# An annealed order of work, bf16 weight flips, clock-keeping matmuls and mixing by token pairs in a linear-attention and token-mixing kernel

## The chip, the cores and the metric

The kernel runs on one NeuronCore of a Trainium2 chip. The metric is the device time of one execution in microseconds (us); smaller is better. The engines are named as in the profile: PE (TensorE, matrix products), DVE (VectorE), ACT (ScalarE), POOL (GpSimd) and SP (SyncE, which here only issues DMAs).

## What is computed

Two layers follow each other. The first is a linear attention with a decaying state, for 4 batches, 8 heads, 768 tokens and 48 features per head; the second mixes tokens with two 768x768 matrices and channels with one 384x384 matrix.

```python
for t in range(S):                                   # attention, state is D x D per batch and head
    cur = np.einsum('bhd,bhe->bhde', u[None] * kt, vt)
    y[:, :, t] = np.einsum('bhd,bhde->bhe', rt, state + cur)
    state = w[None, :, :, None] * state + np.einsum('bhd,bhe->bhde', kt, vt)
x = y, heads side by side                            # (4, 768, 384)
theta = x @ w_theta
zr, zi = x * np.cos(theta), x * np.sin(theta)
y = np.einsum('ts,bsd->btd', w_tok_r, zr) + np.einsum('ts,bsd->btd', w_tok_i, zi)
u = x + y
out = u + np.maximum(u @ w_ch, 0.0)
```

## The kernel before

The 768 tokens of a batch are six chunks of 128, taken as three pairs; a pair of a batch is the unit of work, and there are 12 of them. The weights are loaded once.

For a batch, `heads` scales r by powers of w, two heads at a time (`Rw`, L492, on POOL, in batch 0 on DVE), and turns it with flips, which are PE transposes against an identity matrix (L473), into `RT`. For a pair, `attention` scales k into `Kw` (L520, POOL), flips it into `KT`, casts v to bf16 into `vb` (ACT), makes the scores (PE L543, on 64 rows of the array), masks them into `mAT` (DVE L548), makes `PD` (DVE L553) and from it the diagonal term `dg` (PE L561) and `yd` (POOL L568), carries the state along (PE L585 and L593, result `Sb`), and sums all into y (PE L627 and L632). DVE adds y and yd into `x` (L639). Then x is flipped to `xT`, theta is a product with `Wth` (PE L651), ACT makes sine and cosine (L655, L658), DVE makes `zr` (L661) and POOL `zi` (L664). All this is float32 where it is loaded or accumulated and bf16 where it is multiplied on PE.

`mixing` takes a pair of a batch once all of the batch's zr and zi are there: for each of its two chunks 12 products of 128x384 (PE L683, six with `WrT`, six with `WiT`), summed in one PSUM bank, then `un` (DVE L689), flips to `uT`, the channel product with `Wch` (PE L700), `fin` (DVE L704) and one store of 384 KB (SP L708).

The token weights come as rows and are needed as columns: each of the 12 row blocks (384 KB, float32) is flipped by six float32 transposes (PE L456) into a pair of banks, and copied to `WrT` or `WiT`.

PSUM has six slots in this kernel (`SLOTS`): two of two banks and four of one. Loads go into rings of SBUF buffers (ten `ld` buffers for k, v and weights, two `r_f` buffers for r). Nothing here is ordered by the programmer: `Plan` holds every step as a task with its dependencies, a priority, and an estimated duration on each engine that may run it; `Plan.order` plays the estimates forward, each engine taking the ready task of smallest priority, and the instructions are emitted in the resulting order. On the chip each engine, and SP's queue of DMAs, runs its instructions strictly in that order and waits on semaphores. An engine that waits holds up everything that stands behind it in its own order.

Of the kernel before, what the change touches and what calls it, by code (L numbers as in the profile page):

```python
# [22 lines left out]
SLOTS = (2, 2, 1, 1, 1, 1)  # L23


class Task:
    __slots__ = ("opts", "fn", "deps", "prio", "seq", "acq", "uses", "nwait", "users", "ready",
                 "start", "done", "end", "mode", "lock", "eng", "name")


class Plan:
# [7 lines left out]
    cold = 25000.0  # L39
# [6 lines left out]
    def add(self, opts, fn, rd=(), wr=(), prio=0.0, acq=(), use=(), mode=0, lock=False, name=""):  # L46
        t = Task()
        t.opts, t.fn, t.prio, t.mode, t.lock, t.name = opts, fn, prio, mode, lock, name
        t.seq = len(self.tasks)
# [24 lines left out]

    def pick_banks(self, acq, free, now, kept):
# [12 lines left out]
    def order(self):  # L88
        for t in self.tasks:
            t.users, t.nwait, t.ready = [], len(t.deps), {e: 0.0 for e in t.opts}  # L90
# [5 lines left out]
        def wake(t):  # L96
            for e in t.opts:
                waiting[e].append(t)
# [11 lines left out]
        while len(out) < n:  # L110
            for e in ENGINES:
                while free_at[e] <= now:
                    best, got = None, None
                    kept = set()
                    for t in sorted(waiting[e], key=lambda t: (t.prio, t.seq)):
                        if t.ready[e] > now or (t.lock and port > now):
                            continue
                        if len(t.opts) > 1:
                            mine = now + t.opts[e][0]
                            if any(max(free_at[o], t.ready[o], now) + t.opts[o][0] < mine  # L120
                                   for o in t.opts if o != e):
# [15 lines left out]
                    for o in t.opts:  # L137
                        waiting[o].remove(t)
# [4 lines left out]
                    if e == PE:  # L143
                        if t.mode != last_mode:
                            ns += 80.0
                        last_mode = t.mode
                        if now < self.cold:
                            ns *= 1.6
                    if t.lock:
# [39 lines left out]
def act_op(n, psum=True, ptr=False):  # L189
    return (n / 1.2 + (85 if psum else 100) + (90 if ptr else 0), 135)  # L190


def dve_op(n, rate=1.0):
    return (n / (0.96 * rate) + 70, 115)


def pool_op(n, rate=1.8):
    return (170 + rate * n, 100)


def pe_op(ns):
    return (ns, 215)
# [3 lines left out]
def kernel(  # L206
# [15 lines left out]
    ctx.enter_context(tc.manual_schedule())  # L222
    for t in P.order():
# [3 lines left out]
def build(ctx, tc, nc, r, k, v, w, u, moe_w_theta, moe_w_tok_r, moe_w_tok_i, moe_w_ch, out):  # L227
# [39 lines left out]
    pi2 = sb.tile([C, 1], F32, name="pi2")  # L267
    w_row = sb.tile([1, HD], F32, name="w_row")
# [39 lines left out]
    def setup():  # L308
# [6 lines left out]
        def fills(e):  # L315
            nc.vector.memset(ones, 1.0)
# [3 lines left out]
            for t in Sbs:  # L320
                nc.vector.memset(t, 0.0)
# [3 lines left out]
        P.add({DVE: (600, 100)}, fills, wr=["ones", "wu", "pi2", "uw", "bmask", "Sb0"], prio=-200)  # L325
# [81 lines left out]
    def load_r(b, parts=1):  # L407
        n = H // parts
        for i in range(parts):
            h = slice(i * n, (i + 1) * n)  # L410
            load(3500 / parts, r_fs[b % NR][:, h],
# [9 lines left out]
    def load_kv(b, pr, src):  # L421
        i = slot()
        for c in range(2):
            t0 = (2 * pr + c) * C
            load(1080, Ls[i][:, c, :, :D], src[b, :, t0:t0 + C, :].transpose([1, 0, 2]),
# [9 lines left out]
    def square(src, dst, key, prio, pos=None):  # L435
        s3 = src.rearrange("(o p) n -> p o n", p=C)
        for o, n in ((0, 2), (2, 1)):
            i = slot()
            load(560 * n, flat(i)[:, :n * HD].rearrange("p (o c) -> p o c", o=n),
# [324 lines left out]
```

## Time and profile before

| | |
|---|---|
| time, median of 3 runs | 161.48 us (159.95, 161.48, 161.77) |
| time of the profiled execution | 159.55 us |
| span of the profiled execution, first to last instruction | 157.8 us |
| busy time in that span: PE, DVE, ACT, POOL | 135.1, 110.0, 76.3, 75.6 us |
| moved by DMA | 25.0 MB, of which 20.06 MB read from HBM and 4.72 MB written |

The span is measured by the profiler from the first instruction to the last, and the execution's own time is 1.75 us longer. Matmuls are pipelined, so a PE that is shown busy can still be working slower than it could: a group of matmuls is better judged by the distance from its start to the start of the next group. The granted clock is the share of its full rate at which PE was let run, by the profiler's records.

### The profile page before, as it was taken

Reading aid. Unit: us, or ns where it says so; the run is one execution under the profiler, and the core shown is the slowest. Engines: PE = TensorE matmul, PEld = TensorE weight load, DVE = VectorE, ACT = ScalarE, POOL = GpSimd, SP = SyncE. Lnnn points to the kernel's source line nnn. Section 1 sums busy time; section 2 is a strip of 40 time slices with the busy share of each in tenths; the row PEclk is TensorE's granted clock in tenths of the full one; section 3 lists DMA queues with packets and bytes.
Section 4 is the critical chain, followed back from the end, with each engine's and each line's share of the span. In section 5 each row is a group of like instructions: output and inputs, shape, how many; then the busy total and the mean of one; then the engine's idle time right before and its main releaser. Section 6 shows DMA issues by size and latency. Waiting matters only on the chain.

```text
span 157.8 us, 3653 instructions
## 1 busy us (share of the span) xinstructions
PE 135.1 (86%) x1491; PEld 94.8 (60%) x1491; DVE 110.0 (70%) x158; ACT 76.3 (48%) x119; POOL 75.6 (48%) x61
## 2 busy tenths in 40 slices
PE   4068596788899999999979969999999999999950
PEld 1056474657787676668846737668567676566620
DVE  7196798624622889996999957657996975555540
ACT  3977236348988465747943465516317354000000
POOL 7000730759796564974599976900712442100000
PEclk9999997869999999999999999999999999999996
DMA  4999999999799999999999960202200022021022
GB/s 145 266 224 187 163 265 397 368 397 344 246 165 167 149 186 205 185 166 199 330 175 230 159 102 0 103 19 82 103 1 4 0 102 103 1 100 73 27 100 100
DMA packets 59962, 25.00 MB, mean 158 GB/s; under 512 B 50473, under 2 KB 58410, under 8 KB 59946
## 3 DMA queue, kind: packets, MB, share of 16 engines
q1 hardware_dynamic: 59920, 24.78, 72.9%
q8 instruction: 11, 0.18, 0.5%
q14 instruction: 5, 0.04, 0.1%
q10 hardware_dynamic: 26, 0.00, 0.0%
HBM read 20.06 MB, written 4.72 MB: 157 GB/s over the span
## 4 chain that ended last, share of the span: by engine, by line
PE 49%; DMA 14%; DVE 11%; POOL 9%; SPq 9%; issue 3%; ACT 2%; ACTq 0%; POOLq 0%; DVEq 0%
PE bank L683 22%; DMA r_f<-in_r_dram 11%; SPq L404 8%; PE bank L473 7%; PE bank L700 6%; POOL Rw L492 5%; PE bank L456 4%; DMA ld<-in_k_dram 4%; PE bank L651 3%; POOL Kw L520 3%; DVE zr L661 2%; PE bank L543 2%; DVE PD L553 2%; DVE mAT L548 1%; DVE un L689 1%
## 5 line engine op out<-in xcount | busy, mean ns | idle before, releaser
L683 PE MATMUL bank<-zi,WiT 128*128 128x384 bf16 x144 | 29.7, 326 | 0.0
L683 PE MATMUL bank<-zr,WrT 128*128 128x384 bf16 x144 | 29.2, 326 | 0.0
L548 DVE TENSOR_TENSOR mAT<-bank,mask 128x1024 bf16<-128x1024 f32 x24 | 28.7, 1213 | 0.1
L520 POOL TENSOR_TENSOR Kw<-ld,wpinv 128x768 bf16<-128x768 f32 x10 | 18.6, 1861 | 19.8 <-DMA ld<-in_k_dram 16.8
L664 POOL TENSOR_TENSOR zi<-x,sin 128x768 bf16<-128x768 bf16 x12 | 20.6, 1715 | 15.2 <-ACT sin L655 15.2
L568 POOL TENSOR_TENSOR yd<-dg,vb 128x768 bf16<-128x768 f32 x12 | 17.6, 1472 | 21.1 <-ACT dg L259 16.3
L689 DVE TENSOR_TENSOR un<-bank,x 128x384 bf16<-128x384 f32 x24 | 13.2, 552 | 6.7 <-PE bank L683 6.7
L651 PE MATMUL bank<-Wth,xT 128*128 128x384 bf16 x72 | 15.4, 357 | 2.8 <-DVE xT L261 1.4
L492 POOL TENSOR_TENSOR Rw<-r_f,wpow 128x576 bf16<-128x576 f32 x12 | 16.5, 1405 | 2.2 <-DMA r_f<-in_r_dram 2.2
L639 DVE TENSOR_TENSOR x<-bank,yd 128x768 bf16<-128x768 f32 x12 | 11.4, 953 | 8.6 <-PE bank L632 5.1
L683 PEld LDWEIGHTS <-WiT 128*128 128x128 bf16 x144 | 12.9, 98 | 7.1
L683 PEld LDWEIGHTS <-WrT 128*128 128x128 bf16 x144 | 12.8, 97 | 7.0
L259 ACT ACTIVATE vb<-ld 128x768 bf16<-128x768 f32 x12 | 10.1, 845 | 11.8 <-DMA ld<-in_v_dram 11.3
L704 DVE SCALAR_TENSOR_TENSOR fin<-bank,un 128x768 f32<-128x768 f32 x12 | 11.5, 956 | 6.2 <-PE bank L700 6.2
L655 ACT ACTIVATE sin<-bank 128x768 bf16<-128x768 f32 x12 | 9.7, 810 | 12.0 <-PE bank L651 6.5
L259 ACT ACTIVATE RT<-bank 128x768 bf16<-128x768 bf16 x16 | 12.0, 816 | 4.7 <-PE bank L473 4.6
L700 PE MATMUL bank<-Wch,uT 128*128 128x384 bf16 x72 | 13.7, 326 | 0.7 <-DVE uT L261 0.7
L661 DVE TENSOR_TENSOR zr<-bank,x 128x768 bf16<-128x768 f32 x12 | 11.4, 950 | 2.9 <-ACT bank L658 2.9
L651 PEld LDWEIGHTS <-xT 128*128 128x128 bf16 x72 | 7.3, 104 | 8.2 <-issue 2.7
L543 PE MATMUL bank<-RT,KT 64*128 64x128 bf16 x192 | 9.8, 229 | 2.1 <-ACT KT L259 0.6
L658 ACT ACTIVATE bank<-bank,pi 128x768 f32<-128x768 f32 x12 | 10.5, 873 | 0.0
L473 PE MATMUL bank<-ident,Kw 128*128 128x128 bf16 x96 | 8.4, 241 | 1.9 <-POOL Kw L520 1.7
(79 smaller groups left out, 213.0 us busy)
## 6 DMA issues: line engine op xcount, KB each, us to landing
ld<-in_k_dram SPq DMA_DIRECT2D x24, 192.0 KB, 5.6
ld<-in_v_dram SPq DMA_DIRECT2D x24, 192.0 KB, 5.2
out_dram<-fin SPq DMA_DIRECT2D x12, 384.0 KB, 2.5
r_f<-in_r_dram SPq DMA_DIRECT2D x3, 1152.0 KB, 9.1
ld<-in_moe_w_tok_r_dram SPq DMA_DIRECT2D x6, 384.0 KB, 7.2
ld<-in_moe_w_tok_i_dram SPq DMA_DIRECT2D x6, 384.0 KB, 8.4
r_f<-in_r_dram SPq DMA_DIRECT2D x2, 576.0 KB, 4.7
ld<-in_moe_w_theta_dram SPq DMA_DIRECT2D x1, 384.0 KB, 5.0
```

The lines of the kernel that those rows point to most:

```text
L259: nc.scalar.activation(dst, src, Act.Copy)
L473: nc.tensor.matmul(bank16(tok)[:, i * C:(i + 1) * C], s, ident, is_transpose=True, start=(i == 0), stop=(i == n - 1))
L492: eng_of[e].tensor_mul(Rw[:, :, 2 * hp:2 * hp + 2, :D].transpose([0, 2, 1, 3]), rf[:, 2 * hp:2 * hp + 2, :].rearrange("p h (n d) -> p h n ...
L520: eng_of[e].tensor_mul(Kw[:, :, :, :D].rearrange("p a h d -> p (a h) d"), Ls[ik][:, :, :, :D].rearrange("p a h d -> p (a h) d"), wpinv.rea ...
L548: P.add({DVE: dve_op(8 * C)}, lambda e, tk=tk, c=c: nc.vector.tensor_mul(mAT[:, c].rearrange("p a h t -> p (a h) t"), dbl(tk).rearrange("p ...
L568: P.add({POOL: pool_op(2 * HD, 1.7)}, lambda e: nc.gpsimd.tensor_mul(yd.rearrange("p a (h d) -> p (a h) d", h=H), wide(dg, D), vb.rearrang ...
L651: nc.tensor.matmul(dbl(th)[:, t, :HD], xT[:, ND * t + dk, :], Wth[:, dk, :], start=(dk == 0), stop=(dk == ND - 1))
L661: P.add({DVE: dve_op(2 * HD)}, lambda e: nc.vector.tensor_mul(zr[:, 2 * pr:2 * pr + 2], dbl(th)[:, :, :HD], x[:, 2 * pr:2 * pr + 2]), use= ...
L664: P.add({POOL: pool_op(2 * HD, 1.9)}, lambda e: nc.gpsimd.tensor_mul(zi[:, 2 * pr:2 * pr + 2], x[:, 2 * pr:2 * pr + 2], sn), rd=xk + [("si ...
L683: nc.tensor.matmul(bank(tm)[:, :HD], WT[:, so, to * C:(to + 1) * C], z[:, so], start=(part == 0 and j == 0), stop=(part == 3 and j == 2))
L689: P.add({DVE: dve_op(HD)}, lambda e, tm=tm, t=t, to=to: nc.vector.tensor_add(un[:, t], bank(tm)[:, :HD], x[:, to]), use=[tm], rd=[("x", zj ...
L700: nc.tensor.matmul(dbl(tf)[:, t, :HD], uT[:, ND * t + dk, :], Wch[:, dk, :], start=(dk == 0), stop=(dk == ND - 1))
```

## The change

1. **A table of numbers, `TUNE`**, gives each of 711 tasks an addition to its priority and a mask of the engines that may run it; `Plan.tune` applies it before `Plan.order`. The table was found by annealing over the span that the planner itself foresees. Some of the planner's estimates are changed as well (the time during which PE counts as slow from 25 to 11 us, latencies, load times). More tasks than before may run on another engine: casts of v and of the token weights on POOL, `yd`, `zi`, `Kw` and `Rw` on DVE.
2. **Weight flips in bf16**: each block of token weights is first cast to bf16, in place, in the load's buffer (`Wcast`, on ACT, DVE or POOL), and then flipped by six bf16 transposes into one bank.
3. **Clock-keeping matmuls**: 110 tasks of two 128x128 matmuls of zeros (`warm_up`, the tile `zeros`), each with the lowest priority, so that the planner puts one wherever it foresees PE idle.
4. **Mixing by token pairs**: the 12 products of a chunk are split into six parts of two, each of which needs the zr or zi of one pair and not all of the batch.
5. y is made in two tasks, one for each chunk; the last pair of all is finished and stored in two halves; the memsets of the state buffers come in a task of their own, behind the others.

```diff
+NWARM = 110
+TUNE = {
+    0: (1875, 4), 1: (3287, 4), 2: (-70, 2), 3: (954, 2), 4: (-59, 2), 5: (1547, 2), 6: (340, 4),
...
+    def tune(self, table):
+        for seq, (more, mask) in table.items():
+            t = self.tasks[seq]
+            t.prio += more
+            t.allow = tuple(e for i, e in enumerate(ENGINES) if mask >> i & 1)
...
-                load(1100, flat(i)[:, :S], src[to * C:(to + 1) * C, :], L2(i))
+                load(1040, flat(i)[:, :S], src[to * C:(to + 1) * C, :], L2(i))
...
-                def flip(e, i=i, tok=tok):
-                    for g in range(2):
-                        for j in range(3):
-                            o = (3 * g + j) * C
-                            nc.tensor.matmul(dbl(tok)[:, g, j * C:(j + 1) * C],
-                                             flat(i)[:, o:o + C], ident_f, is_transpose=True,
-                                             start=(j == 0), stop=(j == 2))
-                P.add({PE: pe_op(660)}, flip, rd=L2(i) + ["ident_f"], acq=[(tok, 2)],
+                P.add({ACT: act_op(S, False), DVE: dve_op(S, 2.0), POOL: pool_op(S, 0.9)},
+                      lambda e, i=i, half=half: copy(
+                          e, half, flat(i)[:, :S].rearrange("p (g c) -> p g c", g=2)),
+                      rd=L2(i), wr=L2(i), prio=prio + to, lock=SHARED, allow=(ACT, POOL),
+                      name="Wcast")
+                def flip(e, half=half, tok=tok):
+                    for j in range(NCH):
+                        nc.tensor.matmul(bank16(tok)[:, j * C:(j + 1) * C],
+                                         half[:, j // 3, (j % 3) * C:(j % 3 + 1) * C], ident,
+                                         is_transpose=True, start=(j == 0), stop=(j == NCH - 1))
+                P.add({PE: pe_op(340)}, flip, rd=L2(i) + ["ident"], acq=[(tok, 1)],
...
-            for part in range(4):
+            for part in range(2 * NP):
                 def mix(e, tm=tm, to=to, part=part):
-                    WT, z = ((WrT, zr), (WiT, zi))[part // 2]
-                    for j in range(3):
-                        so = 3 * (part % 2) + j
+                    WT, z = ((WrT, zr), (WiT, zi))[part % 2]
+                    for so in (part // 2 * 2, part // 2 * 2 + 1):
                         nc.tensor.matmul(bank(tm)[:, :HD], WT[:, so, to * C:(to + 1) * C],
...
-                P.add({PE: pe_op(490)}, mix, rd=zk + [(n, to) for n in ("WrT", "WiT")],
+                P.add({PE: pe_op(325)}, mix, rd=[(("zr", "zi")[part % 2], zj, part // 2),
+                                                 (("WrT", "WiT")[part % 2], to)],
...
+        parts = [(0, 2)] if g < B * NP - 1 else [(0, 1), (1, 2)]
...
+    def warm_up():
+        for i in range(NWARM):
+            def warm(e):
+                for _ in range(2):
+                    nc.tensor.matmul(bank("warm")[:, :C], zeros, zeros, start=True, stop=True,
+                                     skip_group_check=True)
+            P.add({PE: (115, 217)}, warm, rd=["zeros"], acq=[("warm", 1)] if i == 0 else [],
+                  use=[] if i == 0 else ["warm"], wr=[] if i == 0 else ["warm"], prio=1e4 + i,
+                  name="warm")
```

What stands where is shown at three places. The rows are an engine's instructions in the order in which it runs them: the line, the operation, result and operands (with buffer numbers), the shape of the result.

**PE at the program's start, before.** `w_row` is the row of decays, `wu` the block that holds w and u, `Rw0` the first scaled r:

```order
L363 MATMUL bank2_63<-w_row_72,ones_70 128x384
L378 MATMUL bank3_64<-ident_f_67,wu_73 128x8
L473 LDWEIGHTS Rw0_97
L473 MATMUL bank4_65<-ident_68,Rw0_97 128x128
L473 LDWEIGHTS Rw0_97
```

**PE at the same place, after the change:**

```order
L870 LDWEIGHTS zeros_72
L870 MATMUL bank2_63<-zeros_72 128x128
L509 MATMUL bank3_64<-w_row_73,ones_70 128x384
L524 MATMUL bank4_65<-ident_f_67,wu_74 128x8
L870 LDWEIGHTS zeros_72
```

Twelve matmuls of zeros now stand ahead of the first product, 44 between the `wu` product and the first flip of `Rw0`; in all 218 of the 220 stand ahead of the third x flip of batch 0.

**DVE where the three x of batch 0 end, before.** `x0` is the x of batch 0, and the row with `yd2` makes its third pair; the rows down to the casts of the first weight columns:

```order
L639 TENSOR_TENSOR x0_126<-bank1_62,yd1_124 128x768
L661 TENSOR_TENSOR zr0_128<-bank0_61,x0_126 128x768
L261 COPY xT1_135<-bank5_66 128x768
L548 TENSOR_TENSOR mAT2_115<-bank1_62,mask01_69 128x1024
L639 TENSOR_TENSOR x0_126<-bank0_61,yd2_125 128x768
L661 TENSOR_TENSOR zr0_128<-bank1_62,x0_126 128x768
L261 CAST WiT_145<-bank1_62 128x6x128
L661 TENSOR_TENSOR zr0_128<-bank0_61,x0_126 128x768
```

**DVE at the same place, after the change** (`yd1`, `zi0`, a scaling of r for batch 1 and a cast of a weight block, `ld6`, are on DVE now):

```order
L716 TENSOR_TENSOR yd1_125<-dg1_122,vb1_104 128x768
L787 TENSOR_TENSOR x0_127<-bank0_61,yd1_125 128x768
L751 TENSOR_TENSOR Sb1_118<-bank5_66,bmask_83 128x384
L402 COPY WrT_145<-bank4_65 128x6x128
L809 TENSOR_TENSOR zr0_129<-bank1_62,x0_127 128x768
L787 TENSOR_TENSOR x0_127<-bank0_61,yd2_126 128x768
L643 TENSOR_TENSOR Rw0_98<-r_f1_97,wpow_79 128x2x6x48
L402 COPY xT0_135<-bank5_66 128x768
L812 TENSOR_TENSOR zi0_131<-x0_127,sin1_134 128x768
L402 CAST ld6_92<-ld6_92 128x2x384
```

The masks now all stand ahead of the last x, one zr does too, and weight columns are copied between them.

**SP where the last loads are issued, before** (`out_0` rows are stores of a finished pair, the third of which is the first row here):

```order
L708 DMA out_0_dram<-fin0_140 128x2x384
L404 DMA ld7_92<-in_k_dram 128x8x48 x2
L404 DMA ld8_93<-in_v_dram 128x8x48 x2
L404 DMA ld9_94<-in_k_dram 128x8x48 x2
L404 DMA ld0_85<-in_v_dram 128x8x48 x2
```

**SP at the same place, after the change** (the first row is the fourth store):

```order
L861 DMA out_0_dram<-fin1_142 128x2x384
L550 DMA ld6_92<-in_v_dram 128x8x48
L550 DMA ld5_91<-in_k_dram 128x8x48
L550 DMA ld9_95<-in_k_dram 128x8x48
L550 DMA ld0_86<-in_v_dram 128x8x48
L550 DMA ld9_95<-in_k_dram 128x8x48
L550 DMA ld7_93<-in_k_dram 128x8x48
L550 DMA ld0_86<-in_v_dram 128x8x48
L550 DMA ld7_93<-in_k_dram 128x8x48
L550 DMA ld8_94<-in_v_dram 128x8x48 x2
```

Ten half loads of k and v now stand behind the fourth store, where eight stood behind the third; halves of different loads are interleaved.

169 lines of the change are left out of this document (91 added, 78 removed), and 123 rows, old and new, of the table TUNE.

## The prediction

> **What bounds the kernel now.** I read first where the busy time lies, then stretches of ten microseconds, then PE's own rows, then the chain of waits.
>
> ```profile
> PE 135.1 (86%) x1491; PEld 94.8 (60%) x1491; DVE 110.0 (70%) x158; ACT 76.3 (48%) x119; POOL 75.6 (48%) x61
> DMA  4999999999799999999999960202200022021022
> 20.00:30.00 10.00, 7.53 (x98) 5.38 (x96) 8.27 (x12) 5.33 (x8) 3.54 (x3) 0.83 1.11 343
> ```
>
> PE is busy for 86% of the span. The second row (DMA share in 40 slices of 3.95 us) is full until slice 23, so loads arrive until about 93 us. In the stretch of 20 to 30 us (columns: PE, PEld, DVE, ACT, POOL, granted clock, DMA share, GB/s) PE is idle for a quarter and runs at 0.83 of its clock. How much of the span PE needs follows from what its work costs at full rate; the chain of waits (start, length, what) gives the prices, since there one group starts where the last ends:
>
> ```profile
> 44.31 1.31 PE bank L456 x12
> ...
> 105.88 2.12 PE bank L473 x38
> 108.00 0.17 PE bank L585 x4
> ...
> 110.70 0.18 PE bank L561 x8
> ...
> 112.08 0.33 PE bank L543 x8
> 112.41 0.59 PE bank L683 x3
> ...
> 115.67 0.20 PE bank L632 x8
> ...
> 137.60 3.41 PE bank L683 x21
> ```
>
> A product of 384 columns costs 3.41/21 = 0.162 us, a bf16 flip 0.056, a float32 weight flip 0.109, a product of 96 columns 0.0425, one of 48 columns 0.025, a dg product 0.0225. Three mixing products cost 0.59 behind scores instead of 0.49, so a change of the array's shape costs 0.1; with one ahead of them eight scores cost 0.22. The sum over 432 wide products (70.2), 336 flips (18.8), 72 weight flips (7.9), 192 scores (5.3), 42 changes of shape (4.4), 160 products of 96 columns (6.8), 192 of 48 (4.8), 96 of dg (2.2) and 8 carries of the state (1.3, as wide ones) is **121.6 us**. The span has 36 more. I divide it at one event, the flip of the third x of batch 0:
>
> ```profile
> 8.81 1.44 PE L473 MATMUL bank<-ident,Rw 128*128 128x128 bf16 x12 [1.51 <-DVE Rw L492]
> 22.22 0.51 PE L473 MATMUL bank<-ident,x 128*128 128x128 bf16 x6
> 32.46 2.08 PE L651 MATMUL bank<-Wth,xT 128*128 128x384 bf16 x6 [0.71 <-DVE mAT L548]
> 36.97 0.51 PE L473 MATMUL bank<-ident,x 128*128 128x128 bf16 x6 [0.77 <-DVE x L639]
> 94.06 1.15 PE L651 MATMUL bank<-Wth,xT 128*128 128x384 bf16 x6 [1.41 <-DVE xT L261]
> 152.11 1.15 PE L700 MATMUL bank<-Wch,uT 128*128 128x384 bf16 x6 [0.65 <-DVE uT L261]
> ```
>
> Ahead of 36.97 PE has done 12.4 of its 121.6 us, half as fast as later: twelve flips take 1.44 us at 8.81 (six take 0.51 at 22.22 as at 36.97, so the slow start ends near 22), and theta takes 2.08 at 32.46 where it takes 1.15 at 94.06. From 36.97 to 153.27, the end of the last product, 116.3 us hold 109.2 of work; **7.1 are lost**, of which 4.4 are idle times in PE's rows (such as the 1.41 at 94.06 and the 0.65 at the end). Behind it come 4.5 us of `fin` and the last store. So there are three levers: the event's time, the work left behind it, and the loss.
>
> **The work left.** Each of the 72 weight flips falls from the float32 price to the bf16 one: 72 x 0.053 = 3.8 us. By the new order there are 38 changes of shape instead of 42, 0.4 less, and 13.1 us stand ahead of the event. Left behind it: 121.6 - 3.8 - 0.4 - 13.1 = 104.3, and two zero matmuls, **104.4 us**. The 12 casts that pay for it go to ACT (8), DVE (2) and POOL (2). A cast on ACT costs as a cast of v:
>
> ```profile
> L259 ACT ACTIVATE vb<-ld 128x768 bf16<-128x768 f32 x12 | 10.1, 845 | 11.8 <-DMA ld<-in_v_dram 11.3
> L568 POOL TENSOR_TENSOR yd<-dg,vb 128x768 bf16<-128x768 f32 x12 | 17.6, 1472 | 21.1 <-ACT dg L259 16.3
> L350 POOL MEMSET Rw<- 128x768 bf16 x1 | 0.7, 737 | 0.0
> ```
>
> Eight times 0.85 is 6.8 us for ACT, which has 80 us idle, and the other half of its v casts leave it. A cast on POOL is not in the trace; it writes what a memset of 0.74 us writes and is at most a product of two operands, 1.47. I take 1.47, the row of the same types: 8 such casts, 8 of `Kw`, 11 `yd`, 7 `zi` and 12 `Rw` come to 72 us on POOL, not more than today's. The cover is thus ACT's and POOL's idle time; without it a late cast would delay a flip, by up to 1.5 us each.
>
> **The time of the event.** DVE sets it. It starts its first product with r at 7.90 and then works through everything up to the third x:
>
> ```profile
> 2.24 1.07 POOL L350 MEMSET Kw<- 128x256 bf16 x4
> 4.42 3.14 ACT L370 ACTIVATE wpow<-lw_f,tok_f 128x384 f32<-128x384 f32 x6
> 7.90 1.43 DVE L492 TENSOR_TENSOR Rw<-r_f,wpow 128x576 bf16<-128x576 f32 x2
> 35.95 0.96 DVE L639 TENSOR_TENSOR x<-bank,yd 128x768 bf16<-128x768 f32 x1 [3.55 <-POOL Rw L492]
> L548 DVE TENSOR_TENSOR mAT<-bank,mask 128x1024 bf16<-128x1024 f32 x24 | 28.7, 1213 | 0.1
> L639 DVE TENSOR_TENSOR x<-bank,yd 128x768 bf16<-128x768 f32 x12 | 11.4, 953 | 8.6 <-PE bank L632 5.1
> L553 DVE TENSOR_TENSOR PD<-RT,KT 128x1024 bf16<-128x1024 bf16 x12 | 9.2, 775 | 0.1
> ```
>
> In the new order the memsets of `Kw`, `Rw` and the mask stand ahead of POOL's iota, which feeds the exponents of `wpow`: about 2.3 us later, and seven exponents of 3.14/6 = 0.52 us come before the first `Rw`, so DVE starts at about 9.1 instead of 7.9. From there to the third x stand six masks (7.3), three x (2.9), three PD (2.3) and 17 smaller operations (11.3: `Kw`, `Rw`, yd and zr at 0.75 to 0.95, the rest near 0.55), 23.8 by their means, 21.4 since each starts some 0.08 before the one ahead of it ends. In the trace DVE idled 7.3 us there. The 3.55 before the third x go: the profile names a `Rw`, but y itself ended only at 35.8, behind the slow theta of 32.46, and that theta waited for the pair of banks which a weight flip and a mask had held. The weight flips need no pairs any more. I keep the other 3.7 and add 0.8, because half of r now stands behind two loads of k. Event at 9.1 + 21.4 + 4.5 = **35.0 us**.
>
> This needs a fast PE, which is what the zeros are for. Before, the granted clock fell twice ahead of the event, each time just behind an idle PE (columns here: PE busy, clock, DMA share, GB/s):
>
> ```profile
> 25.00:28.40 3.40, 3.00 (x31) 0.58 1.04 392
> 32.00:35.40 3.40, 2.94 (x24) 0.55 1.03 397
> 7.06 0.24 PE L378 MATMUL bank<-ident_f,wu 8*128 8x8 f32 x1 [3.20 <-DMA wu<-in_u_dram]
> ```
>
> Behind the product of `wu`, which still waits for its DMA until 7.06, 44 zeros run without a pause, at the slow price (0.11) about 4 us, so the first flips start near 11.2 and not at 8.8; DVE has its r only at 9.1 to 12, so this costs PE and not the event. The stretches say that one idle window costs some 3.4 us of half clock. [...]
>
> **Loss and tail.** Of the 7.1 us I keep the 2.7 that stand in no idle row, and half of the 4.4, since mixing parts can start with one pair and fill gaps; 0.6 more for the joint below: **5.5** (bounds: 2.7 if no gap remains, 12 if the gaps are those of before and again as much). Behind the last product `fin` of one chunk costs 0.55 like `un` instead of 0.96, and its store is half as long: 3.9 instead of 4.5.
>
> **The joint** is a second, independent bound. SP stops at a store until its `fin` is there, and the last ten half loads stand behind the fourth store.
>
> ```profile
> 86.04 2.28 SPq L404 DMA_DIRECT2D ld<-in_k_dram  x2
> L520 POOL TENSOR_TENSOR Kw<-ld,wpinv 128x768 bf16<-128x768 f32 x10 | 18.6, 1861 | 19.8 <-DMA ld<-in_k_dram 16.8
> ```
>
> By the prices, PE ends the fourth store's product 43.1 us of work behind the event; with 2 of loss at 80, `fin` 81. Ten halves of 1.14 us end at 92.5, land some 2.5 later, POOL needs 1.9 for the last `Kw`: 97. PE reaches the flips of that `Kw` with 60.9 us of work, at 98. So it fits by 1 us, and from there 43.5 us of work remain: the end of PE cannot come much before 97 + 43.5 = 140.5. An order that were better elsewhere would meet this.
>
> **Sum:** 35.0 + 104.4 + 5.5 + 3.9 = 148.8 us of span, and with the 1.75 between span and time 150.5, against 159.55 for the profiled execution. That execution is 1.2% below the median of 161.48; the runs lie 0.3 to 1.4% above it, so I add half of 1.2% and predict **151.5 us**, 6% faster.
>
> **Rivals.**
> 1. *The plan does not hold on the chip.* The order is fitted to foreseen times, and each engine keeps to it even when a step is late. For it: the event, the loads and POOL meet within 1 us. Against: PE holds 104 us of work ahead and each other engine has 20 us to spare. Losses of 11 to 13 give 157 to 159.
> 2. *DVE and POOL block each other.* DVE gets five `zi`, two `Kw`, one `yd` and two casts that read SBUF, as POOL does.
>
> ```profile
> 58.94 1.21 DVE L553 TENSOR_TENSOR PD<-RT,KT 128x1024 bf16<-128x1024 bf16 x1
> 76.91 0.68 DVE L553 TENSOR_TENSOR PD<-RT,KT 128x1024 bf16<-128x1024 bf16 x1
> 78.29 2.13 POOL L664 TENSOR_TENSOR zi<-x,sin 128x768 bf16<-128x768 bf16 x1 [1.61 <-ACT sin L655]
> ```
>
> A `PD` costs 0.68 while POOL is idle and 1.21 beside a `Kw`. Ten such meetings at 0.5 are 5 us, which DVE (93 us of work in 108 behind the event) can still take; at a wait of up to half of a `Kw`, 0.9, and the same for the nine `PD`, 17, it cannot, and PE loses some 4 more: 155. [...]
> 3. *The zeros do not hold the clock, until it comes by itself at 22 us* as in the trace. Ahead of the event stand 13.1 us of work and 218 zeros, 12.4. If PE is slow until time c, the event comes at 28.3 + c/2: at 22, 39.3, 4.3 late, which gives 156.
> 4. *Slower than before*, by the same mechanism and place: the zeros are instructions, and the work behind them waits. From c = 36.6 on, the event lies at 46.6 or later and the time at 163 or more, 1% slower. For it: in the two falls of 25 and 32 us PE shows 3.0 and 2.9 us busy of 3.4, and stays slow to the end of the stretch. Against: the clock was released at 22 by less dense work.
>
> **Chances.** Forecast (147 to 154) 0.58; rival 1 0.20 (a quarter of it within 1%); rival 2 0.08; rival 3 0.06; rival 4, or anything that makes it slower, 0.08. One per cent is about what a measurement of this kernel can tell from no change: faster 0.87, within 1% 0.05, slower 0.08. The range of 8 in 10 goes from the joint's floor (140.5 + 3.9 + 1.75 = 146) to the middle of rival 1, 158.5.
>
> **What would show it.** The third x flip near 35 us with theta at about 1.1 us; granted clock 1.00 from about 12 us; weight flips at 0.056; last loads landed at 94 to 96; PE full from 40 us on, with idle rows of together 2 to 3 us; the end 4 us behind the last product. Wrong would be a clock below 0.9 after 15 us, a DVE that waits for POOL's operands ahead of the third x, or SP waiting at a store while the DMA share falls before 90 us.

## The result, and the profile after

The changed kernel takes **153.12 us** (median of four runs, 152.98 to 154.07), beside 160.71 (159.41 to 161.77) for the kernel before on the same chip: a ratio of **0.954, interval 0.945 to 0.964**. Two of the four runs of the kernel before (161.48 and 161.77) are as long as those that later measurements of it count as slow; beside the other two the ratio is 0.96. Forecast were 151.5 us and a range of 146 to 158.5.

By the terms of the forecast, in the profiled execution (153.25 us, span 151.5):

| us | before | forecast | after |
|---|---|---|---|
| flip of the third x of batch 0 | 36.97 | 35.0 | 36.43 |
| PE work left behind it, by the prices | 109.2 | 104.4 | 104.4 |
| lost behind it | 7.1 | 5.5 | 7.1 |
| from the last product's end to the span's end | 4.5 | 3.9 | 3.5 |
| span | 157.8 | 148.8 | 151.5 |

The last product ends at 147.96, so 111.5 us follow the event and 7.1 of them are lost. Of the 6.3 us that the span shrank, 4.8 are PE work that no longer stands behind the event (4.2 spared, the rest now done ahead of it), 1.0 the shorter tail, 0.5 the event; the loss is what it was. This only adds up the span; which of it is a cause, the experiments ask.

The page of the changed kernel, its rows on busy time and on the DMA share in 40 slices of 3.8 us:

```profile
PE 138.2 (91%) x1711; PEld 100.1 (66%) x1711; DVE 117.3 (77%) x170; ACT 81.0 (53%) x124; POOL 70.3 (46%) x61
DMA  5999998999789999899999699902011200023205
```

DVE has 7.3 us more to do than before, POOL 5.3 less, and loads arrive until about slice 26, 98 us, some 5 us later. Stretches of the changed kernel (PE, PEld, DVE, ACT, POOL busy, granted clock, DMA share, GB/s):

```profile
30.00:40.00 10.00, 8.82 (x127) 7.20 (x125) 8.54 (x11) 9.93 (x13) 6.36 (x5) 1.00 0.92 299
80.00:90.00 10.00, 8.25 (x95) 5.35 (x94) 8.46 (x10) 4.69 (x9) 7.74 (x6) 1.00 0.97 201
90.00:100.00 10.00, 9.91 (x174) 7.97 (x175) 9.29 (x13) 6.01 (x12) 8.63 (x7) 1.00 1.13 142
```

PE has two wide gaps: at 30 to 40 us, where ACT is full, and at 80 to 90. From 90 us on it is full. PE's rows (start, length, in brackets the idle time before and what ended it):

```profile
11.73 0.88 PE L624 MATMUL bank<-ident,Rw 128*128 128x128 bf16 x12
35.46 1.14 PE L799 MATMUL bank<-Wth,xT 128*128 128x384 bf16 x6 [1.18 <-DVE zr L809]
36.43 0.50 PE L624 MATMUL bank<-ident,x 128*128 128x128 bf16 x6
84.74 0.40 PE L691 MATMUL bank<-RT,KT 64*128 64x128 bf16 x8 [0.33 <-DVE fin L857]
86.89 0.35 PE L709 MATMUL bank<-uw,PD 128*128 128x2 bf16 x8 [0.86 <-DVE PD L701]
89.95 0.62 PE L624 MATMUL bank<-ident,Kw 128*128 128x128 bf16 x8 [0.45 <-DVE Kw L669]
103.53 0.61 PE L624 MATMUL bank<-ident,Kw 128*128 128x128 bf16 x8
```

The first flips are fast behind the zeros (0.88 for twelve, where before they took 1.44). The **first gap** ends in the event; ACT's and DVE's rows in front of it:

```profile
31.55 1.28 ACT L803 ACT_TABLE_LOAD   x1
33.55 0.87 ACT L806 ACTIVATE bank<-bank,pi 128x768 f32<-128x768 f32 x1
34.45 0.96 DVE L809 TENSOR_TENSOR zr<-bank,x 128x768 bf16<-128x768 f32 x1 [1.43 <-ACT bank L806]
35.33 0.95 DVE L787 TENSOR_TENSOR x<-bank,yd 128x768 bf16<-128x768 f32 x1
```

The new order puts a zr ahead of the third x on DVE. That zr waits 1.43 us for ACT's cosine, and ACT, full with casts and copies, first loads its table for sines, 1.28 us. Much earlier, a Kw on DVE has already taken 1.60 instead of 0.95, beside an Rw of POOL:

```profile
12.38 1.91 POOL L643 TENSOR_TENSOR Rw<-r_f,wpow 128x576 bf16<-128x576 f32 x1 [8.66 <-DMA r_f<-in_r_dram]
13.50 1.60 DVE L669 TENSOR_TENSOR Kw<-ld,wpinv 128x768 bf16<-128x768 f32 x1 [0.48 <-DMA ld<-in_k_dram]
```

In the **second gap** DVE is late; DVE's and POOL's rows there:

```profile
83.73 0.96 DVE L857 SCALAR_TENSOR_TENSOR fin<-bank,un 128x768 f32<-128x768 f32 x1 [1.54 <-DMA out_dram<-fin]
85.07 1.76 DVE L701 TENSOR_TENSOR PD<-RT,KT 128x1024 bf16<-128x1024 bf16 x1
87.90 2.00 DVE L669 TENSOR_TENSOR Kw<-ld,wpinv 128x768 bf16<-128x768 f32 x1
82.16 4.13 POOL L643 TENSOR_TENSOR Rw<-r_f,wpow 128x576 bf16<-128x576 f32 x3 [0.95 <-DMA r_f<-in_r_dram]
87.61 1.47 POOL L716 TENSOR_TENSOR yd<-dg,vb 128x768 bf16<-128x768 f32 x1 [1.32 <-ACT dg L400]
```

`fin` waits for its buffer's store; then PD (0.68 alone) takes 1.76 and Kw (0.95 alone) 2.00, each while a product of POOL runs. PE's waits of 0.86 and 0.45 are for exactly these two.

### The profile page after: what moved, and what is told of

The parts are those of the page before. It is cut to its first block, busy times and chain, and to the rows that moved or that the text cites. A ratio compares the mean times of both kernels' runs of the same rounds, so it can differ in the third digit from the quotient of the medians.

```text
span 151.5 us, 4089 instructions
## 1 busy us (share of the span) xinstructions
PE 138.2 (91%) x1711; PEld 100.1 (66%) x1711; DVE 117.3 (77%) x170; ACT 81.0 (53%) x124; POOL 70.3 (46%) x61
## 4 chain that ended last, share of the span: by engine, by line
PE 46%; DMA 15%; SPq 10%; DVE 9%; issue 7%; ACT 7%; POOL 2%; ACTq 0%; DVEq 0%
PE bank L830 23%; SPq L550 10%; DMA ld<-in_v_dram 8%; PE bank L852 6%; PE bank L624 6%; DMA out_dram<-fin 5%; PE bank L799 3%; DMA ld<-in_moe_w_tok_i_dram 3%; PE bank L691 2%; DVE Kw L669 2%; PE bank L778 2%; ACT sin L803 2%; DVE fin L857 1%; DVE zr L809 1%; DVE zi L812 1%
## 5 line engine op out<-in xcount | busy, mean ns | idle before, releaser
L830 PE MATMUL bank<-zr,WrT 128*128 128x384 bf16 x144 | 34.4, 326 | 0.7 <-DVE WrT L402 0.7
L830 PE MATMUL bank<-zi,WiT 128*128 128x384 bf16 x144 | 34.5, 326 | 0.0
L716 POOL TENSOR_TENSOR yd<-dg,vb 128x768 bf16<-128x768 f32 x11 | 16.5, 1505 | 19.3 <-DVE dg L402 9.9
L870 PE MATMUL bank<-zeros 128*128 128x128 bf16 x220 | 18.8, 242 | 1.9 <-DVE zeros L465 1.9
L669 POOL TENSOR_TENSOR Kw<-ld,wpinv 128x768 bf16<-128x768 f32 x8 | 14.8, 1848 | 10.6 <-DMA ld<-in_k_dram 10.6
L857 DVE SCALAR_TENSOR_TENSOR fin<-bank,un 128x768 f32<-128x768 f32 (+1 forms) x13 | 11.6, 894 | 7.9 <-PE bank L852 6.3
L812 POOL TENSOR_TENSOR zi<-x,sin 128x768 bf16<-128x768 bf16 x7 | 11.5, 1638 | 12.9 <-ACT sin L803 12.9
L870 PEld LDWEIGHTS <-zeros 128*128 128x128 bf16 x220 | 15.5, 110 | 2.3 <-DVE zeros L465 1.9
L400 ACT ACTIVATE uT<-bank 128x768 bf16<-128x768 bf16 (+1 forms) x8 | 5.7, 727 | 17.2 <-PE bank L624 17.2
L400 ACT ACTIVATE KT<-bank 128x1024 bf16<-128x1024 bf16 x9 | 9.2, 1023 | 7.4 <-PE bank L624 6.6
L701 DVE TENSOR_TENSOR PD<-RT,KT 128x1024 bf16<-128x1024 bf16 x12 | 9.6, 802 | 1.5 <-ACT RT L400 1.3
```

What stands on the lines that cost most here:

```text
L400: nc.scalar.activation(dst, src, Act.Copy)
L669: eng_of[e].tensor_mul(Kw[:, :, :, :D].rearrange("p a h d -> p (a h) d"), Ls[ik][:, :, :, :D].rearrange("p a h d -> p (a h) d"), wpinv.rea ...
L716: P.add({POOL: pool_op(2 * HD, 1.7), DVE: dve_op(2 * HD)}, lambda e: eng_of[e].tensor_mul(yd.rearrange("p a (h d) -> p (a h) d", h=H), wid ...
L812: P.add({POOL: pool_op(2 * HD, 1.9), DVE: dve_op(2 * HD, 2.0)}, lambda e: eng_of[e].tensor_mul(zi[:, 2 * pr:2 * pr + 2], x[:, 2 * pr:2 * p ...
L830: nc.tensor.matmul(bank(tm)[:, :HD], WT[:, so, to * C:(to + 1) * C], z[:, so], start=(so == 0 and part == 0), stop=(part == 2 * NP - 1 and ...
L857: nc.vector.scalar_tensor_tensor(fin[:, lo:hi], dbl(tf)[:, :hi - lo, :HD], 0.0, un[:, lo:hi], op0=Alu.max, op1=Alu.add), use=[tf], rd=uk, ...
```

## The experiments

Each takes a part of the change away or adds one; edits are to the changed kernel unless said. Below, "foreseen" is the planner's own span, the last end in its plan.

**Without the table.** Edit:

```diff
-    P.tune(TUNE)
```

> The changed kernel without the table of numbers: bf16 flips, zeros, mixing by pairs, split y and halves stay, the planner orders them by its plain priorities. Theory (PE's queue sets the time, and of the 6.3 us won only 0.5 came from the event and nothing from the loss, so the order itself is worth little): 153 to 156 us. Rival (the order found by annealing carries the gain): 158 to 161 us, with a loss behind the third x flip of 12 us or more, or an event later than 38 us.

Measured: **150.78 us** (150.35 to 151.26), ratio 0.948 (0.942 to 0.955). Both expectations miss: without the annealed table the kernel is faster, by 2.2 us beside the next three experiments, which keep the table and ran on the same chip (152.99 to 153.76). Stretches of it, and its and the changed kernel's group of Kw on DVE:

```profile
30.00:40.00 10.00, 9.42 (x113) 6.53 (x111) 7.14 (x9) 8.65 (x12) 9.48 (x8) 1.00 1.07 374
80.00:90.00 10.00, 10.00 (x147) 7.25 (x146) 9.52 (x13) 7.09 (x13) 8.54 (x6) 1.00 1.19 172
L668 DVE TENSOR_TENSOR Kw<-ld,wpinv 128x768 bf16<-128x768 f32 x3 | 2.9, 951 | 0.0
L669 DVE TENSOR_TENSOR Kw<-ld,wpinv 128x768 bf16<-128x768 f32 x4 | 5.5, 1376 | 0.5 <-DMA ld<-in_k_dram 0.5
```

Both gaps are smaller or gone, POOL has the work that the table gives to DVE (all twelve `zi`, for one), and a Kw on DVE takes 0.95, not 1.38. The event itself comes later than in the changed kernel, at 37.57, but by the prices 16.3 us of PE's work are done ahead of it, against some 13: between different orders, the time of the event alone says little.

**Without the zeros**, same order:

```diff
-                for _ in range(2):
+                for _ in range(0):
```

> The changed kernel with the same order, but the 220 matmuls of zeros are left out. Theory (the zeros hold the clock and PE's latency is part of the chain to the third x): granted clock falls to about 0.55 for one or two stretches of 3.4 us between 12 and 40 us, the third x flip comes at 38.5 to 41 us instead of 36.4, time 155.5 to 158. Rival (DVE and ACT set the event, a slow PE hides behind them): event 36 to 37, time 152.5 to 153.5.

Measured: **153.01 us** (152.76 to 153.9), ratio 0.963 (0.957 to 0.969), no different from the changed kernel. PE's rows and a stretch:

```profile
23.68 0.81 PE L608 MATMUL bank<-ident,ld 128*128 128x128 bf16 x6
27.23 0.49 PE L624 MATMUL bank<-ident,x 128*128 128x128 bf16 x6
35.50 0.50 PE L624 MATMUL bank<-ident,x 128*128 128x128 bf16 x6
32.00:36.00 4.00, 1.83 (x27) 1.38 (x25) 2.48 (x3) 3.97 (x6) 3.21 (x3) 1.00 1.05 294
```

PE is slow until some 25 us (0.81 for six flips at 23.68, 0.49 at 27.23), and yet the event comes at 35.50, 0.9 earlier than with the zeros. DVE and ACT set it, not a slow PE. The 0.9 are what the zeros themselves cost at the program's start. First two rows of the changed kernel, then the same two without the zeros:

```profile
3.25 1.64 PE L509 MATMUL bank<-w_row,ones 1*128 1x384 f32 x2
9.14 1.43 DVE L643 TENSOR_TENSOR Rw<-r_f,wpow 128x576 bf16<-128x576 f32 x2 [1.44 <-ACT wpow L516]
2.36 1.61 PE L509 MATMUL bank<-w_row,ones 1*128 1x384 f32 x2 [2.36 <-DMA w_row<-in_w_dram]
8.21 1.43 DVE L643 TENSOR_TENSOR Rw<-r_f,wpow 128x576 bf16<-128x576 f32 x2 [0.57 <-ACT wpow L516]
```

ACT's exponents for `wpow` need the product of `w_row`, and in the changed kernel twelve zeros run ahead of it; without them DVE starts on r 0.93 earlier. The end hardly follows, though: the median time is 0.1 shorter.

**Every weight flip twice**, 72 flips more at 0.056, 4.0 us of work for PE:

```diff
-                    for j in range(NCH):
+                    for j in [*range(NCH), *range(NCH)]:
```

> The changed kernel with each of the 72 bf16 weight flips issued twice (same result): 4.0 us more PE work, 1.7 of it ahead of the third x flip, where PE has zeros to give, and 2.4 behind it. Theory (behind the event every microsecond of PE work lengthens the time): 155.2 to 157 us. Rival (loads, stores and DVE set the pace up to the last Kw at 103 us and PE has slack there): 153 to 154 us.

Measured: **152.99 us** (152.2 to 154.39), ratio 0.963 (0.956 to 0.971). The rival holds. All doubled flips stand between 24 and 51 us, and their work vanishes into PE's gaps:

```profile
80.00:90.00 10.00, 9.75 (x116) 6.70 (x114) 9.12 (x12) 4.70 (x9) 9.50 (x6) 1.00 1.03 249
102.46 0.61 PE L624 MATMUL bank<-ident,Kw 128*128 128x128 bf16 x8
```

PE is full where it was idle, and reaches the last flips of Kw 1.1 us earlier, not later: here DVE loses less beside POOL (the Kw that took 2.00 at 87.90 takes 1.03 at 87.88, 0.17 ahead of a `yd` of POOL that takes 2.19).

**A third buffer for `fin`**, in a tile of the setup, made larger for it, that is dead by then:

```diff
...
-    fins = ring(2, [C, 2, HD], F32, "fin")
+    fins = ring(2, [C, 2, HD], F32, "fin") + [lw_big]
...
-        un, uT, fin = uns[g % 2], uTs[g % 2], fins[g % 2]
+        un, uT, fin = uns[g % 2], uTs[g % 2], fins[g % 3]
```

> The changed kernel with a third buffer for fin (g modulo 3 instead of 2; it shares memory with the decay logarithms of the setup), order as before. Before, the fourth fin waited 1.54 us at 83.7 us for the third store, which lay behind a 1152 KB load of r. Theory (that wait is passed on to PD, Kw and to PE, 3.3 us lost between 84 and 95 us): 151.5 to 152.4 us, the loss between 84 and 95 us falls to about 2. Rival (the time is set elsewhere, the wait only moves): 152.9 to 153.4 us.

Measured: 153.76 us (152.59 to 154.08), ratio 0.966 (0.960 to 0.971): outside both ranges, and no gain. The store goes out 0.8 earlier (83.96 instead of 84.72), but the same engine is late one step on:

```profile
83.96 0.38 SPq L862 DMA_DIRECT2D out_dram<-fin  x1
89.55 2.19 DVE L702 TENSOR_TENSOR PD<-RT,KT 128x1024 bf16<-128x1024 bf16 x1 [0.16 <-ACT KT L400]
```

**The sine table loaded early**:

```diff
...
+        def last_exp(e):
+            nc.scalar.activation(wR, lw_p, Act.Exp, scale=float(REF))
+            nc.scalar.preload_act_table_set("trig_and_small")
...
```

> The changed kernel, its order and its zeros as they are; only ACT's table of sine values is loaded right behind the last exponential and not in front of the first sine at 31.55 us, where it took 1.28 us while ACT was busy for 9.93 of 10 us. Theory (PE has no slack behind the event, so the event sets the end): zr and the third x come 1.2 us earlier, the flip of the third x stands at 35.2 instead of 36.43, and the time falls from 153.1 to 151.9. Rival (doubling the weight flips cost nothing, so PE has slack up to some 90 us, and what DVE, POOL and the loads deliver between 75 and 92 us sets the end): the event comes earlier, the end doesn't: 152.7 to 153.3.

Measured: **151.57 us** (151.39 to 152.19), ratio 0.955 (0.951 to 0.960). The times lie wholly below those of the changed kernel, but were taken on another chip; the ratios, taken against different runs of the kernel before, cannot tell them apart. The trace bears the times out, with a span of 149.9:

```profile
9.96 1.28 ACT L534 ACT_TABLE_LOAD   x1
33.15 0.96 DVE L811 TENSOR_TENSOR zr<-bank,x 128x768 bf16<-128x768 f32 x1
35.20 0.50 PE L626 MATMUL bank<-ident,x 128*128 128x128 bf16 x6
```

The event is at 35.20, as expected, 1.23 earlier, and the last product's end 1.6 earlier. So here the end follows the event, as the theory has it. It need not: without the zeros the event came 0.9 earlier, DVE's and ACT's work with it, and the end hardly moved.

**Half of the table**: engines as in the table, order by the planner's own priorities:

```diff
-            t.prio += more
```

> The changed kernel with half of its table: each task may run only on the engines that the table names, but the order follows the planner's own priorities. The planner then foresees a span of 147.6 us, against 142.0 with the whole table and 144.1 without any. Theory (the table's placement, which gives DVE some Kw, zi, yd and casts that POOL would do, costs time by itself: DVE is the busiest engine beside PE and its operations stretch beside POOL's): 152 to 156, above the 150.8 of the kernel without the table. Rival (placement is harmless, the table's order is what loses): 150 to 151.5.

Measured: **155.4 us** (155.12 to 155.57), ratio 0.978 (0.974 to 0.983), as the theory has it: placement alone costs 4.6 us beside the kernel without the table. A row of PE and a group of DVE:

```profile
67.16 0.51 PE L623 MATMUL bank<-ident,Rw 128*128 128x128 bf16 x6 [1.08 <-POOL Rw L642]
L715 DVE TENSOR_TENSOR yd<-dg,vb 128x768 bf16<-128x768 f32 x3 | 4.1, 1361 | 0.0
```

PE waits for a scaled r, and three `yd` on DVE take 1.36 on average, 4.1 in sum, though the one at 107.33 takes 0.94. The one on DVE in the changed kernel takes 0.95. The table's order wins back part of what its placement loses.

**Neither table nor zeros**, the first two edits together:

```diff
-    P.tune(TUNE)
...
-                for _ in range(2):
+                for _ in range(0):
```

> The planner's own order as in the kernel without the table, and of the tasks of zeros nothing is emitted. Theory (the zeros are worth nothing once the flips and the mixing have no long idle stretch left): 150.3 to 151.3, the granted clock 1.00 at 24 to 36 us, and the early flips slow until about 14 us. Rival (in this order the idle stretches of the kernel before come back, and with them the two falls of the clock, each 3.4 us at half speed): clock 0.8 to 0.9 between 20 and 40 us and 153 to 154.5.

Measured: **150.82 us** (150.01 to 150.9), ratio 0.949 (0.944 to 0.954). The time is the theory's, the clock the rival's:

```profile
16.00:20.00 4.00, 2.67 (x37) 2.26 (x37) 3.73 (x5) 0.84 (x1) 1.35 (x1) 0.60 1.50 163
20.00:24.00 4.00, 3.77 (x48) 3.08 (x46) 3.42 (x5) 1.84 (x5) 0.79 (x1) 0.55 1.19 283
32.00:36.00 4.00, 4.00 (x38) 2.73 (x37) 2.58 (x4) 3.02 (x5) 2.52 (x4) 0.77 1.04 397
```

The clock falls to 0.55 and 0.77, PE does about 1 us less by 36 us than with the zeros, and the end is the same.

**The kernel before with flips and pairs alone**; the edit is to the kernel before, the cast only on ACT:

```diff
-                P.add({PE: pe_op(660)}, flip, rd=L2(i) + ["ident_f"], acq=[(tok, 2)],
+                P.add({ACT: act_op(S, False)},
...
+                P.add({PE: pe_op(340)}, flip, rd=L2(i) + ["ident"], acq=[(tok, 1)],
...
-            for part in range(4):
+            for part in range(2 * NP):
```

> The kernel before with two parts of the change alone: weight flips in bf16 behind a cast on ACT, and mixing in parts of one token pair; no table, no zeros, y and the last store as before. Theory (the gain is the work that PE is spared, 4.2 us, and nothing else of weight): 155 to 156, a ratio of 0.97 to 0.975. Rival 1 (the weight flips stand where PE has slack, as doubling them cost nothing): 158 to 159.5, a ratio of 0.99 to 1.00. Rival 2 (these two parts carry all of it, also by filling gaps and freeing pairs of banks early): 151 to 153.5, a ratio of 0.95 to 0.962.

Measured: 157.72 us (156.69 to 157.99), ratio 0.989 (0.985 to 0.994): nearly the first rival's. The flips now wait for their casts:

```profile
33.09 0.51 PE L461 MATMUL bank<-ident,ld 128*128 128x128 bf16 x6 [2.47 <-ACT ld L259]
```

**The same with the new numbers in the planner**:

```diff
-    cold = 25000.0
+    cold = 11000.0
...
-    return (n / 1.2 + (85 if psum else 100) + (90 if ptr else 0), 135)
+    return (n / 1.2 + (50 if psum else 100) + (90 if ptr else 0), 175)
```

> The kernel before with bf16 weight flips (cast on ACT) and mixing by pairs, 157.7 us, and now also with the changed kernel's numbers in the planner (times of operations, loads and the slow start, taken from a trace); the planner foresees 147.5 us. Theory (what the kernel without the table has over the flips and pairs, 6.9 us, is the planner's numbers: with them it places the work so that fewer waits arise): 151 to 153.5. Rival (numbers as close as before's change little; the 6.9 us come from the casts that POOL may take, y in two tasks, the halved last store): 156.5 to 158.5.

Measured: 157.13 us (155.69 to 158.14), ratio 0.990 (0.984 to 0.996): the rival. PE is ahead up to 60 us and then loses it:

```profile
60.00:70.00 10.00, 8.05 (x121) 5.81 (x118) 7.59 (x8) 6.62 (x11) 9.59 (x7) 1.00 1.27 209
70.45 0.34 PE L565 MATMUL bank<-uw,PD 128*128 128x2 bf16 x8 [1.99 <-ACT RT L259]
```

**Neither table nor zeros nor pairs**:

```diff
-            for part in range(2 * NP):
+            for part in range(4):
...
-                P.add({PE: pe_op(325)}, mix, rd=[(("zr", "zi")[part % 2], zj, part // 2),
-                                                 (("WrT", "WiT")[part % 2], to)],
+                P.add({PE: pe_op(490)}, mix, rd=zk + [(n, to) for n in ("WrT", "WiT")],
```

> The kernel without table and zeros, 150.8 us, with mixing as before the change: four parts of three products, each of which waits for zr and zi of all three pairs of the batch. Theory (mixing by pairs gives PE work to fill gaps with ahead of the third x, where it had done 14.8 us of work at 36 us against 12.3): PE does 2 to 3 us less work up to 40 us and the time is 153 to 155. Rival (the gaps fill with other work): 150.3 to 151.8.

Measured: **156.13 us** (155.44 to 156.35), ratio 0.986 (0.983 to 0.989): pairs are worth 5.3 us here (5.9 by the ratios; the two kernels ran on different chips), more than the theory's 153 to 155. PE waits early, with nothing to fill the wait (1.5 us less work done at 40 us):

```profile
30.83 0.40 PE L690 MATMUL bank<-RT,KT 64*128 64x128 bf16 x8 [2.06 <-DVE zr L808]
50.75 0.35 PE L708 MATMUL bank<-uw,PD 128*128 128x2 bf16 x8 [1.45 <-DVE PD L700]
```

**Neither table nor zeros, y of a pair in one task**:

```diff
-        for c in range(2):
-            def outputs(e, c=c, cc=2 * pr + c):
+        def outputs(e):
+            for c in range(2):
...
+        P.add({PE: pe_op(740)}, outputs, rd=rt_keys + [kM + (0,), kM + (1,), kv_, S_mid] +
```

> The kernel without table and zeros, 150.8 us, with y of a pair in one task again, as before the change: it then needs both masks and the middle state at once, where the first chunk's y now needs one mask and the state before. The planner foresees 149.0 us instead of 144.1; in the runs so far that were planned without the table, the measured span lay 3.6 to 7.8 us above the foreseen one, with 5.0 for the kernel without table and zeros. Theory (y in halves carries most of what the flips and the pairs alone had not brought): span 153 to 155, time 154.5 to 157. Rival (y in halves is of no weight, and the casts that POOL takes, or the sum of all small edits, carries it): 150.3 to 152.

Measured: **155.29 us** (154.61 to 156.76), ratio 0.983 (0.976 to 0.990), span 153.1: the theory. That is 4.5 us more by times on two chips, 5.5 by the ratios. PE is ahead up to 90 us and then has nothing ready:

```profile
90.00:100.00 10.00, 7.31 (x101) 6.15 (x99) 5.60 (x9) 5.99 (x10) 5.65 (x4) 0.85 0.43 54
96.05 0.49 PE L623 MATMUL bank<-ident,Rw 128*128 128x128 bf16 x6 [2.15 <-ACT RT L399]
```

**The best of them: no table, sine table early**:

```diff
-    P.tune(TUNE)
...
+            nc.scalar.preload_act_table_set("trig_and_small")
```

> The kernel without the table (150.8 us), with ACT's sine table loaded right behind the last exponential, as it gained 1.5 us with the table. Theory (the event bounds in this order too): 149.3 to 150.0. Rival (here the load of the table already lies in an idle time of ACT, or PE has other work while it lasts): 150.4 to 151.2.

Measured: **149.55 us** (148.85 to 150.4), ratio **0.946** (0.942 to 0.949), span 147.7: the theory. At 90 to 100 us PE and POOL are full:

```profile
90.00:100.00 10.00, 9.95 (x115) 7.18 (x114) 8.18 (x11) 7.19 (x10) 10.00 (x7) 1.00 0.47 93
```

It is 3.6 us below the changed kernel, by times on two chips. With the early sine table, the annealed table costs 2.0 us (151.57 against 149.55, also on two chips; 1.5 by the ratios).

Two tables sum this up. The first has PE's work done by a time: every product counted at its start in the trace, at the forecast's prices, the zeros left out.

| us of work by | 40 | 60 | 90 | 105 | 140 |
|---|---|---|---|---|---|
| before | 15.3 | 33.8 | 61.8 | 75.2 | 109.7 |
| changed kernel | 16.2 | 34.8 | 60.7 | 75.0 | 109.9 |
| no table | 18.8 | 36.0 | 63.8 | 78.2 | 113.1 |
| no table, no zeros | 17.8 | 35.8 | 63.5 | 78.2 | 112.9 |
| no table, no zeros, y in one | 19.4 | 38.2 | 65.4 | 74.8 | 109.0 |
| no table, no zeros, no pairs | 16.3 | 33.5 | 60.0 | 74.9 | 108.1 |
| no table, sine table early | 19.3 | 37.5 | 64.9 | 79.6 | 114.4 |

The changed kernel does its work hardly sooner than the kernel before; it has less to do. The kernels without the table are 2 to 3 us ahead of it at 40 us if they mix by pairs, and stay ahead if y is in halves. And what the planner foresaw:

| span, us | foreseen | measured | beyond |
|---|---|---|---|
| before (older numbers in the planner) | 151.2 | 157.8 | 6.6 |
| before, flips and pairs (older numbers) | 148.4 | 156.2 | 7.8 |
| before, flips, pairs, new numbers | 147.5 | 154.0 | 6.5 |
| changed kernel | 142.0 | 151.5 | 9.5 |
| changed kernel, sine table early | 142.0 | 149.9 | 7.9 |
| no table | 144.1 | 149.0 | 4.9 |
| no table, sine table early | 144.1 | 147.7 | 3.6 |
| engines of the table only | 147.6 | 153.5 | 5.9 |
| no table, no zeros, no pairs | 148.1 | 154.2 | 6.1 |
| no table, no zeros, y in one | 149.0 | 153.1 | 4.1 |

The table gains 2.1 us in the plan; the chip adds 4.6 more to that order than to the plain one, so it ends 2.5 behind. The losses without pairs and with y in one task, 4.0 and 4.9 us in the plan, do show on the chip.

## Why the prediction was right, and where it was not

The total was right within 1.6 us, for reasons of which about half hold.

- **The work left** held to the number, 104.4: the count was known from the program, and the price of 0.056 for a bf16 weight flip was right. But the step that took spared work one for one as spared time was too simple: 4.0 us of extra flips cost nothing where the weight flips stand, at 24 to 51 us, since PE later waits for DVE and ACT anyway. That PE's work counts from where PE is full, 90 us on, is likely, but no run doubled work there.
- **The event** was 1.4 us too early, and the term that was mis-sized is DVE's work up to the third x: 22.7 us in the trace, not 21.4. One Kw took 0.65 longer beside POOL, and the operations overlapped by 1.6 in all, not by 2.4. Two terms were right by luck. DVE's start was 9.14 as forecast, but not because of the late iota: the numbers made from it (`tok_f`) are ready at 3.95 us, as early as before, and the exponents wait for the product of `w_row` behind twelve zeros. DVE's waits were 4.5 in sum as forecast, but 1.43 of them stand before a zr, for ACT, where the forecast had kept the old waits and not asked what ACT does. With ACT's table load moved, the event stood at 35.20. And 44 zeros at 0.11 are 4.8 us, not the 4 written there (4.87 in the trace); that moved only PE's first flips, to 11.73.
- **"This needs a fast PE"** was wrong. Without zeros PE was slow until 25 us and the event came no later. What the third and fourth rivals feared, zeros that take PE's time and still leave it slow, did not come about (0.88 for the first twelve flips), so their prices are untested. Where the clock did fall, in the kernel without table and zeros, the end did not move.
- **The loss** was 7.1 and not 5.5. Gaps of PE did not halve; they moved to 84 to 90 us, to a DVE that works beside POOL. The rival of two engines that block each other had the right mechanism. By the groups, Kw (four at 1.38 instead of 0.95), zi (five at 0.87 instead of 0.56) and PD (twelve at 0.80 instead of 0.68) are 4.7 us longer on DVE than alone; without the table it is 1.8, all of it in PD (0.83).
- **The joint** slipped from 98 to 103.5 us and was not what bound: PE reached the last Kw late and did not wait for it, though the last load landed only at 100.2, not at 94 to 96. From there the 43.5 us of work took 44.4.
- **The cast on POOL** was taken at 1.47, the upper bound; the traces show 0.83 (changed kernel, two at 827 ns). The error was on the safe side and hid nothing.
- **The tail** was 3.5, not 3.9. **The half of 1.2%** added between the profiled execution and the median was not there: the profiled execution of the changed kernel lies 0.1 above its median. Without it the forecast would have been 150.5, 2.6 below.
- **That the plan does not hold** had 0.20 and was half true: 9.2 us foreseen (between plans with different numbers), 6.3 got, and an order that is 2 us worse than the planner's own.

What carries the gain, then, is not the annealed order and not the zeros. Undone one at a time from the kernel without table and zeros, the pairs cost 5.3 us and the halves of y 4.5. The forecast had priced the pairs at 2.2, half of the 4.4 of idle time, and the halves of y not at all. Added to the kernel before, flips and pairs bring only about 1%. The parts seem to need each other: by the traces, pairs give PE work early, and halves of y keep work ready while the last loads arrive. Each edit also makes the planner lay out everything anew, so these numbers are those of an edit with its plan, not of the edit alone.

Open is how the table's remaining 2.0 us divide between its placement and its order; the placement with the plain order costs 4.6, but the order with the plain placement was not tried. Open is what the bf16 flips bring, since no run undid them alone. Open too is which of the small edits (casts that POOL may take, the task of zeros in the plan, the halved last store) make up the rest.

## What to carry to other kernels

An order that is searched on a model fits the model's errors: compare it on the chip with the plain order of the same planner, and distrust a gain in the plan that is smaller than the scatter of what the chip adds to a plan (here 3.6 to 6.5 us in the orders that were not searched and used the new numbers: a gain of 2.1 was lost in it, losses of 4.0 and 4.9 were not). Before spared work is counted as spared time, ask in which stretch the engine is full; the cheap test is to double the work. A finer grain of tasks (pairs, halves) can be worth more than any order of coarse ones, and its parts may show nothing when tried alone.

## What the runs showed of the hardware

**DVE waited out POOL's instruction.** In the changed kernel a Kw on DVE that starts at 87.90, 0.29 behind a `yd` of POOL (87.61 to 89.08), ends at 89.90, that is 0.82 behind the end of the `yd`. A PD shows the same in the kernel without zeros:

```profile
76.29 2.24 DVE L701 TENSOR_TENSOR PD<-RT,KT 128x1024 bf16<-128x1024 bf16 x1
76.17 1.81 POOL L669 TENSOR_TENSOR Kw<-ld,wpinv 128x768 bf16<-128x768 f32 x1 [0.88 <-DMA ld<-in_k_dram]
```

It starts 0.12 behind the Kw of POOL, which ends at 77.98, and ends 0.55 later. The 2.24 are what was left of the Kw, 1.69, and most of the 0.68 of a PD alone. The trace of the kernel before shows the same: the PD at 58.94 ends at 60.15, some 0.55 behind a Kw of POOL that ran from 57.79 to 59.61. The forecast had weighed waits of up to half of a Kw, 0.9. Masks, which read PSUM, kept their 1.21 beside POOL (in the kernel before the one at 55.07, beside a `yd` of POOL from 55.01).

**The load of an activation table took 1.28 us**, twice in each of four traces (the kernel before, the changed kernel, without the table of numbers, and with the sine table early). No further wait stands beside the load in front of the sine: in the changed kernel ACT's copy ends at 31.53, the load runs from 31.55 to 32.83, and the sine begins at 32.84.

**The granted clock does not show the slow start.** Two stretches of the kernel without zeros:

```profile
16.00:20.00 4.00, 2.56 (x42) 1.85 (x39) 3.96 (x5) 1.76 (x2) 1.81 (x1) 1.00 1.49 171
20.00:24.00 4.00, 3.73 (x56) 3.24 (x55) 3.54 (x6) 3.29 (x5) 2.71 (x2) 1.00 1.04 315
```

It reads 1.00, while the six flips at 23.68 above take 0.81 and not 0.50. And with PE busy for 2.56 of 4 us it reads 1.00 at 16 to 20, while without table and zeros it reads 0.60 there with PE busy for 2.67: the share of busy time in a stretch does not tell whether the clock falls. In the kernel before, by stretches of 0.2 us, it reads about 0.50 from 25.5 to 28.9 us and from 32.4 to 35.8, behind idle times of PE of 0.63 and 0.71; behind one of 1.12, which ends at 30.00, it reads 1.00. So the forecast's 3.4 us of half clock hold for these two falls, but not behind every idle time.
